# Twelve output pairs: issued in front of the second step, or left further behind

## The chip, the cores and the metric

The kernel runs on 1 core of one Trainium2 chip. The metric is device time in microseconds (us), the median of the fast runs where nothing else is said; the profile covers one execution and its span is some 2 us shorter than that execution's time. Executions are compared within the fast state only: two fell into a slow state (one of 1206.62 us, one profile at a granted clock of 0.754) and are left out. In the runs used the granted TensorE clock was 0.999 to 1.0.

## The reference, cut to what matters

```python
# attention part: per head a causal 7-tap convolution over the sequence, with softmaxed taps
out = np.einsum('hk,bskhg->bshg', softmax(weight), windows_of(x))     # 32768 tokens x 192
# second part
h = out @ w_in                      # 192 -> 2048
g = h / (1 + np.exp(-beta * h))     # Swish with one beta for each of the 2048 features
return g @ w_out                    # 2048 -> 192
```

## The kernel before

Work goes in 32 **steps** of 1024 tokens (two halves of 512), each of 16 **units** of 128 features. A unit u of step s does, on TensorE (PE), the *hidden* matmuls (6 of them, into the tile `ph`, of which there are two, in PSUM, the memory in which matmuls accumulate here), then a number of *output pairs*; ScalarE (ACT) turns `ph` into `g`; VectorE (DVE) convolves for a later step and evicts finished output accumulators (it adds up their two halves into the tile `osb`).

An output **job** is 256 tokens of a step's output: 32 pairs of matmuls (16 feature blocks x 2 blocks of 128 tokens) accumulate in one PSUM accumulator, `pa` or `pb`. There is exactly one of each. `ph` twice, `pa` and `pb`, of two 2 KiB banks each, are eight banks: all that the Trainium skill (PSUM — Partial Sum Buffer, Specifications (TRN2)) gives for PSUM, so a third accumulator of this size has no room; that the limit is eight was not tried here.

```python
class Job:
    def ready(self, s, u):
        fcs = NF if self.s < s else max(0, u - LAG + 1)   # LAG = 2: two units behind ScalarE
        return self.done < fcs * self.nb
    ...
    def leave(self):                                      # the eviction
        osb = osb_pool.tile([128, 2, D], FP32, name="osb")
        ...
        nc.vector.tensor_reduce(dst, self.po[:, :, 0 : nb * D].rearrange("p r n -> p n r"),
                                axis=mybir.AxisListType.X, op=ALU.add)
        ...  # then the store to HBM

def output(s, u, pairs, free):
    for _ in range(pairs):
        for name in free:                                 # a freed slot takes the next job
            if slots[name] is None and waiting:
                slots[name] = waiting.popleft()
        live = [(j.s, j.h, j.q, n) for n, j in slots.items() if j is not None]
        for *_, name in sorted(live):                     # the oldest job that is ready goes on
            job = slots[name]
            if job.ready(s, u):
                break
        else:
            return                                        # none ready: this unit gets fewer pairs
        if job.po is None:
            job.po = place[name]()                        # must wait until the last job there is evicted
        if job.pair():                                    # two matmuls; True: it was the last
            job.leave()
            slots[name] = None

for s in range(N_ST):
    jobs_of(s)                                            # 4 jobs, 128 pairs
    for u in range(NF):
        if s == 1 and u == 0:
            output(s, u, 12, "ab")                        # the early run that the change removes
        if s > 0 or u > 1:
            hidden(s, u)
        ...
        if s > 0:
            output(s, u, 8 if s < N_ST - 1 else 7, "ab")
        elif u > 8:
            output(s, u, 5, "ab")
        elif u > 2 and u not in CONV1:
            output(s, u, 4, "a")
        ...                                               # convolution taps, loads, casts
while waiting or any(slots.values()):                     # the tail
    output(N_ST, 0, 1, "ab")
```

A step creates 128 pairs and its 16 units issue 8 each, so the **backlog** (pairs created and not yet issued when a step ends) stays what it is, unless `ready` refuses.

Of the kernel before, what the change touches and what calls it, by code (L numbers as in the profile page):

```python
# [17 lines left out]
def kernel(  # L18
# [72 lines left out]
    def load(ch):  # L91
        p, c = divmod(ch, CHUNKS)
        xf = xf_pool.tile([128, 2, NB, D], FP32, name="xf")
        for h in range(2):
            nc.sync.dma_start(
                out=xf[:, h],
                in_=x_v[p, c * TOK : (c + 1) * TOK, h, :].rearrange(
                    "(b q) d -> q b d", q=BLK
                ),
            )  # L100
        xfs[ch] = xf

    def cast(ch, h):
        if h == 0:
            xbs[ch] = xb_pool.tile([128, NB, NG, 2, DG], BF16, name="xb")
        nc.vector.tensor_copy(  # L106
            xbs[ch][:, :, :, h, :],
            xfs[ch][:, h].rearrange("q b (p c) -> q b c p", c=NG),
        )
# [13 lines left out]
    def xpose(ch):  # L123
        xt = new_xt(ch)
        halo(ch, xts[ch - 1])
        for b in range(NB):
            nc.sync.dma_start_transpose(
                xt[:, :, HALO + b * BLK : HALO + (b + 1) * BLK],
                xbs[ch][:, b].rearrange("q c h p -> q (c h p)"),
            )  # L130
# [242 lines left out]
    def conv_ops(s, c0):  # L373
        def tap(k):
            if k == 0 and c0 == 0:
                new_ct(s)
            o = HALO - PAD + k
            src = xts[s][:, c0:, o : o + TOK]
            dst = cts[s][:, c0:, :]
            scalar = cw[:, k : k + 1]  # L380
            if k == 0:
                nc.vector.tensor_scalar_mul(dst, src, scalar)  # L382
            else:
                nc.vector.scalar_tensor_tensor(  # L384
                    out=dst, in0=src, scalar=scalar, in1=dst, op0=ALU.mult, op1=ALU.add
                )

        return [lambda k=k: tap(k) for k in range(K)]
# [3 lines left out]
    def hidden(s, fc, js=range(NG), ph=None):  # L392
        if fc == 0 and s not in gs:
            gs[s] = g_pool.tile([128, NF, 2, TOK], BF16, name="g")
        if ph is None:
            ph = psum_h.tile([128, 2, TOK], FP32, name="ph")
        for j in js:
            for h in range(2):
                rows = slice(h * DG, (h + 1) * DG)
                nc.tensor.matmul(  # L400
                    ph[:, h, :],
                    w_in_s[rows, j, fc * 128 : (fc + 1) * 128],
                    cts[s][rows, j, :],
                    start=(j == 0),
                    stop=(j == NG - 1),
                )
            if j == NG - 1:
                nc.scalar.activation(  # L408
                    gs[s][:, fc], ph, AF.Silu, scale=beta[:, fc : fc + 1]
                )  # L410
        return ph
# [59 lines left out]
    def jobs_of(s):  # L471
        for h in range(2):
            for q in range(0, NB, 2):
                if s == N_ST - 1 and h == 1 and q == NB - 2:
                    waiting.extend([Job(s, h, q, 1), Job(s, h, q + 1, 1)])
                else:
                    waiting.append(Job(s, h, q, 2))

    def output(s, u, pairs, free):
        for _ in range(pairs):  # L480
            for name in free:
# [4 lines that stand above are left out]
            for *_, name in sorted(live):  # L486
# [4 lines that stand above are left out]
                return  # L491
            if job.po is None:
                job.po = place[name]()
            if job.pair():
                job.leave()
                slots[name] = None
# [10 lines left out]
    for s in range(N_ST):  # L507
        jobs_of(s)
        at = 9 if s == 0 else 0
        for u in range(NF):  # L510
            if s == 1 and u == 0:
                output(s, u, 12, "ab")
            if s > 0 or u > 1:
                hidden(s, u)
            elif u == 0:
                phs = [hidden(0, fc, range(NG - 1)) for fc in range(2)]
                for fc in range(2):
                    hidden(0, fc, range(NG - 1, NG), phs[fc])
            if s == 0 and 0 < u < 4:
                next(second_work)  # L520
            if s == 0 and u in CONV1:
                next(conv1_work)
# [6 lines that stand above are left out]
            if s == 0 and u in first_work:  # L529
                first_work[u]()  # L530

            if s == 0 and u == min(CONV1):
                queue.extend(conv_ops(1, 1))
            pops = u % 2 if s > 0 else u in (4, 6, 7, 9, 11, 12, 13)
            if pops and queue:
                queue.popleft()()

            if u == at and s + 3 < N_CH:
                load(s + 3)
            if u == at and s + 2 < N_CH:  # L540
                cast(s + 2, 0)
            if u == at + 1 and s + 2 < N_CH:
                cast(s + 2, 1)
                xpose(s + 2)
            if u == 12 and s + 2 < N_CH:
                queue.extend(conv_ops(s + 2, 0))
# [32 lines left out]
```

## Time and profile before

| before | |
|---|---|
| time | 702.66 us, the middle of three runs, of which one was slow; the fast runs are 701.54 and 702.66 |
| span of the profile | 699.5 us |
| one unit in full swing | 1.308 us |
| one step (28 steps' mean) | 21.167 us; 16 units would be 20.93 |
| ScalarE per unit | 1.11 us of work, 0.19 us of waiting |

From the page of the kernel before: busy time by engine, the chain of waits that ended last by engine, and four groups of instructions (busy us, mean ns | idle us before, and what ended most of it). PEld is the loading of weights for TensorE, POOL is GpSimd, "issue" is time in which an engine waited for nothing that the profile shows, and ACTq is ScalarE's sequencer.

```profile
PE 690.4 (99%) x11300; PEld 518.3 (74%) x11300; DVE 519.5 (74%) x467; ACT 575.9 (82%) x525; POOL 6.5 (1%) x17
...
PE 92%; DVE 4%; ACT 2%; issue 1%; ACTq 0%
...
L408 ACT ACTIVATE g<-ph,beta 128x1024 bf16<-128x1024 f32 x512 | 569.5, 1114 | 106.1 <-PE ph L400 100.6
L433 PEld LDWEIGHTS <-g 64*128 64x128 bf16 x8160 | 367.7, 94 | 114.3 <-issue 11.2
...
L433 PE MATMUL pa<-w_out_s,g 64*128 64x192 bf16 x4112 | 240.0, 243 | 3.3 <-ACT g L408 1.1
...
L451 DVE TENSOR_REDUCE osb<-pa 128x384 f32<-128x768 f32 x64 | 61.0, 953 | 154.5 <-PE pa L433 154.5
```

PE bounds the kernel, and only 3.3 us of waiting are shown in front of `pa`'s matmuls. The timeline of the kernel before around the start of one step (start us, length us, engine, line, operation, count, then idle time in front):

```profile
351.66 0.51 PE L433 MATMUL pa<-w_out_s,g 64*128 64x192 bf16 x8
...
351.99 0.51 PE L433 MATMUL pb<-w_out_s,g 64*128 64x192 bf16 x8
352.21 0.96 DVE L451 TENSOR_REDUCE osb<-pa 128x384 f32<-128x768 f32 x1 [4.67 <-PE pa L433]
...
352.32 0.83 PE L400 MATMUL ph<-ct,w_in_s 64*128 64x512 bf16 x6
...
353.22 0.84 PE L433 MATMUL pa<-w_out_s,g 64*128 64x192 bf16 x16
353.22 0.60 PEld L433 LDWEIGHTS <-g 64*128 64x128 bf16 x15 [0.37 <-issue]
...
353.87 0.83 PE L400 MATMUL ph<-ct,w_in_s 64*128 64x512 bf16 x6
```

Read the starts, not the lengths. Hidden matmuls are followed by pairs 0.65 us after they start in the units around it; here 352.32 is followed by 353.22, which is 0.25 us late. The lengths overlap (the profile models the end of a matmul), so no idle time is shown in front of the matmuls. What the late one waits for is DVE's eviction of `pa`, from 352.21 to 353.17. The chain of waits of the kernel before, in order of time, says so too:

```profile
351.84 0.34 PE pa L433 x8
...
352.21 0.97 DVE osb L451
...
353.22 0.84 PE pa L433 x16
```

The chain counts the whole eviction, 0.97 us, of which 0.25 are lost.

The start of step 1, in the timeline of the kernel before:

```profile
32.13 0.34 PE L433 MATMUL pa<-w_out_s,g 64*128 64x192 bf16 x4
...
33.10 0.34 PE L433 MATMUL pa<-w_out_s,g 64*128 64x192 bf16 x4 [0.63 <-ACT g L408]
33.28 0.82 PE L433 MATMUL pb<-w_out_s,g 64*128 64x192 bf16 x16
...
33.94 0.81 PE L400 MATMUL ph<-ct,w_in_s 64*128 64x512 bf16 x6
...
34.79 1.11 ACT L408 ACTIVATE g<-ph,beta 128x1024 bf16<-128x1024 f32 x1 [1.75 <-PE ph L400]
```

The early run's first job needs the newest `g`; PE waits for ACT, the hidden matmuls of step 1 stand behind it, and then ACT waits 1.75 us for them. The Trainium skill (PSUM — Partial Sum Buffer, Engine vs sequencer instructions) says that matmuls start in program order; this trace agrees: the ready ones start at 33.94, behind the one that waited to 33.10.

### The profile page before, as it was taken

How to read it: one execution, taken by the hardware profiler on the slowest of the kernel's cores; microseconds unless marked ns; L12 is line 12 of the kernel's file. 1: busy time of each engine (PE TensorE's matmuls, PEld its weight loads, DVE VectorE, ACT ScalarE, POOL GpSimd, SP SyncE). 2: the span in 40 equal slices, each digit the busy share in tenths (PEclk: the TensorE clock that was granted, in tenths of full speed). 3: DMA queues.
4: the chain of work that ended last, by engine and by line, in shares of the span. 5: the costliest groups of instructions: out<-in, count | busy, mean ns of one | idle time of the engine just before them, and what ended most of it. 6: DMA issues, size and time to landing. Idle time of an engine off the chain costs nothing.

```text
span 699.5 us, 24308 instructions
## 1 busy us (share of the span) xinstructions
PE 690.4 (99%) x11300; PEld 518.3 (74%) x11300; DVE 519.5 (74%) x467; ACT 575.9 (82%) x525; POOL 6.5 (1%) x17
## 2 busy tenths in 40 slices
PE   8999999999999999999999999999999999999998
PEld 4677777777777777777777777777777777777776
DVE  5898877797777897777887777987777977778712
ACT  5788888888888888888888888888888888888884
POOL 3000000000000000000000000000000000000000
PEclk9999999999999999999999999999999999999999
DMA  9654322443322443323444423443323443232111
GB/s 212 173 115 115 87 89 73 98 114 107 94 75 75 110 115 100 95 75 76 115 114 99 93 65 89 115 115 86 104 58 98 115 109 87 75 80 65 47 36 58
DMA packets 121445, 66.86 MB, mean 96 GB/s; under 512 B 53232, under 2 KB 121344, under 8 KB 121344
## 3 DMA queue, kind: packets, MB, share of 16 engines
q1 hardware_dynamic: 119632, 63.73, 35.2%
q0 software_dynamic: 1664, 1.57, 1.4%
q8 instruction: 88, 1.44, 0.9%
q14 instruction: 13, 0.11, 0.1%
q10 hardware_dynamic: 48, 0.01, 0.0%
HBM read 29.89 MB, written 25.17 MB: 79 GB/s over the span
## 4 chain that ended last, share of the span: by engine, by line
PE 92%; DVE 4%; ACT 2%; issue 1%; ACTq 0%
PE ph L400 44%; PE pa L433 25%; PE pb L433 22%; DVE osb L451 4%; ACT g L408 2%; PE ph L274 1%; PE pb L274 0%; ACT xt L285 0%; PE pa L274 0%; DVE xt L342 0%; DVE w_out_s L301 0%; PE ph L226 0%; PE pb L243 0%; ACTq L153 0%; ACT L177 0%
## 5 line engine op out<-in xcount | busy, mean ns | idle before, releaser
L408 ACT ACTIVATE g<-ph,beta 128x1024 bf16<-128x1024 f32 x512 | 569.5, 1114 | 106.1 <-PE ph L400 100.6
L433 PEld LDWEIGHTS <-g 64*128 64x128 bf16 x8160 | 367.7, 94 | 114.3 <-issue 11.2
L400 PE MATMUL ph<-ct,w_in_s 64*128 64x512 bf16 x3072 | 423.0, 376 | 0.6 <-ACT g L408 0.6
L384 DVE SCALAR_TENSOR_TENSOR ct<-xt,cw,ct 128x1536 bf16<-128x1536 bf16 (+1 forms) x186 | 333.7, 1794 | 2.3
L433 PE MATMUL pa<-w_out_s,g 64*128 64x192 bf16 x4112 | 240.0, 243 | 3.3 <-ACT g L408 1.1
L433 PE MATMUL pb<-w_out_s,g 64*128 64x192 bf16 (+1 forms) x4048 | 225.4, 243 | 0.0
L400 PEld LDWEIGHTS <-w_in_s 64*128 64x128 bf16 x3072 | 157.3, 94 | 55.1 <-issue 1.8
L451 DVE TENSOR_REDUCE osb<-pa 128x384 f32<-128x768 f32 x64 | 61.0, 953 | 154.5 <-PE pa L433 154.5
L451 DVE TENSOR_REDUCE osb<-pb 128x384 f32<-128x768 f32 x63 | 60.0, 953 | 9.4 <-PE pb L433 7.6
L106 DVE CAST xb<-xf 128x768 bf16<-128x768 f32 x60 | 40.5, 674 | 0.3 <-DMA xf<-in_x_dram 0.3
L382 DVE TENSOR_SCALAR ct<-xt,cw 128x1536 bf16<-128x1536 bf16 (+1 forms) x31 | 30.7, 990 | 0.0
L226 PE MATMUL ph<-zeros 128*128 128x512 bf16 (+3 forms) x12 | 4.5, 476 | 1.3 <-DVE warm L176 1.3
L449 ACT COPY osb<-pb 128x192 f32<-128x192 f32 x1 | 0.3, 319 | 6.1 <-PE pb L433 6.1
L317 ACT ACTIVATE ct<-pa,rn 128x512 bf16<-128x512 f32 x1 | 0.7, 687 | 5.6 <-PE pa L274 5.6
L206 POOL DMA_DIRECT2D w_in_s<-in_moe_w_in_dram x8 | 5.1, 648 | 0.0
L121 DVE COPY xt<-xt 128x18 bf16<-128x18 bf16 x27 | 4.4, 162 | 0.0
L274 PE MATMUL ph<-xt,diag 128*128 128x512 f32 x14 | 3.5, 401 | 0.4 <-ACT xt L285 0.4
L315 DVE TENSOR_SCALAR ct<-ph,rn 128x512 bf16<-128x512 f32 x2 | 1.5, 750 | 3.1 <-PE ph L274 3.1
L301 DVE TENSOR_TENSOR w_out_s<-w_out_raw,beta_r 128x768 bf16<-128x768 f32 x4 | 3.8, 946 | 0.0
L274 PEld LDWEIGHTS ph<-xt,diag 128*128 128x128 f32 x14 | 2.5, 188 | 1.2 <-ACT xt L285 0.6
L342 DVE COPY xt<-pb 128x768 bf16<-128x768 bf16 x2 | 1.9, 958 | 1.5 <-PE pb L243 1.5
L226 PEld LDWEIGHTS <-zeros 128*128 128x128 bf16 x12 | 1.3, 123 | 2.1 <-DVE warm L176 1.3
(53 smaller groups left out, 28.0 us busy)
## 6 DMA issues: line engine op xcount, KB each, us to landing
out_dram<-osb SPq DMA_DIRECT2D x127, 192.0 KB, 2.0
xf<-in_x_dram SPq DMA_DIRECT2D x60, 384.0 KB, 4.4
xt<-xb SPq DMA_TRANSPOSE x120, 3.2
x<-in_x_dram SPq DMA_DIRECT2D x4, 384.0 KB, 5.1
w_in_s<-in_moe_w_in_dram POOLq DMA_DIRECT2D x8, 192.0 KB, 11.7
w_out_raw<-in_moe_w_out_dram SPq DMA_DIRECT2D x4, 384.0 KB, 15.3
out_dram<-osb SPq DMA_DIRECT2D x2, 96.0 KB, 1.6
cw<-in_weight_dram ACTq DMA_DIRECT2D x1, 0.2 KB
```

Of the source, the lines that this page charges most:

```text
L106: nc.vector.tensor_copy(xbs[ch][:, :, :, h, :], xfs[ch][:, h].rearrange("q b (p c) -> q b c p", c=NG),)
L121: nc.vector.tensor_copy(dst, last[:, :, HALO + TOK - PAD :])
L206: nc.gpsimd.dma_start(out=w_in_s[r * DG : (r + 1) * DG, :, cols], in_=w_in_v[:, :, cols])
L226: nc.tensor.matmul(pf[:, 0, 0:cols], zeros[:, 0:128], zeros[:, 0:cols], start=True, stop=True)
L274: nc.tensor.matmul(pv, diag[:, k, :], xt[:, o : o + TOK], start=(k == 0), stop=(k == K - 1))
L301: nc.vector.tensor_tensor(w_out_s[:, fcs, :], w_out_raw[:, fcs, :], beta_r[:, fcs].unsqueeze(2).to_broadcast((128, NQ, D)), ALU.mult,)
L382: nc.vector.tensor_scalar_mul(dst, src, scalar)
L384: nc.vector.scalar_tensor_tensor(out=dst, in0=src, scalar=scalar, in1=dst, op0=ALU.mult, op1=ALU.add)
L400: nc.tensor.matmul(ph[:, h, :], w_in_s[rows, j, fc * 128 : (fc + 1) * 128], cts[s][rows, j, :], start=(j == 0), stop=(j == NG - 1),)
L408: nc.scalar.activation(gs[s][:, fc], ph, AF.Silu, scale=beta[:, fc : fc + 1])
L433: nc.tensor.matmul(self.po[:, r, b * D : (b + 1) * D], g[rows, fc, self.h, q * BLK : (q + 1) * BLK], w_out_s[rows, fc, :], start=(self.don ...
L451: nc.vector.tensor_reduce(dst, self.po[:, :, 0 : nb * D].rearrange("p r n -> p n r"), axis=mybir.AxisListType.X, op=ALU.add,)
```

## The change

The 12 pairs in front of step 1 are not issued early; every later pair is issued as many places further behind the hidden matmuls.

```diff
         for u in range(NF):
-            if s == 1 and u == 0:
-                output(s, u, 12, "ab")
             if s > 0 or u > 1:
                 hidden(s, u)
```

## The prediction

> **What bounds it.** TensorE. The page has PE 99% busy at clock 0.999; the chain of waits is 92% PE. In time order a full unit of work (6 matmuls L400, then 8 output pairs L433) starts every 1.308 us (six starts from 358.44 to 366.29); ScalarE needs 1.11 us per unit and waits 0.19 us for PE each time; VectorE has idle time left (154.5 us waiting for pa). One output pair costs about 0.083 us (40 matmuls in 1.65 us in the tail).
>
> **What is not seen in the busy share.** A step of 16 units takes 21.167 us ((649.55 - 78.05) / 27), not 16 x 1.308 = 20.93. The missing 0.235 us is at one place: at 351.66 pa gets its last 4 pairs and pb its last 4 in the same unit; both accumulators are finished, hidden matmuls follow (0.65 us), and the next pa pair waits for the eviction of pa (352.21 to 353.17) and starts at 353.22 instead of 352.97. The chain shows it once per step as "DVE osb 0.97". The idle column misses it, since modelled matmul ends cover it; the Trainium skill (Perfetto Trace Analysis, Identifying the Most-Contended Engine) calls matmul busy time a bad measure for this reason, and the trace agrees.
>
> **Why.** I counted the issue order. Before, the 12 early pairs leave the backlog so small that in step 1 the rule "two units behind" starves the last units (7 and 4 pairs instead of 8), and the backlog locks at 72 pairs per step end, where both first jobs of a step end together in unit 0 of the next. Without the 12, the backlog stays at 79: 8 pairs in every unit; pa ends in unit 0 and pb still has 4 + 7 pairs. So between pa's last pair and its reuse lie 0.33 + 0.65 + 0.58 = 1.56 us, where the eviction took 1.23 us from end to restart (351.99 to 353.22). No other accumulator change of the step is closer. The pair that reads the newest g (units 14, 15) stands where it stood.
>
> **Cost.** Matmuls, evictions, bytes: unchanged; only order. The tail gets 7 pairs longer (95 instead of 88, +0.58 us), which is work taken from before it, so not a loss. Gains, all on PE:
> - 28 stalls of 0.235 us at the starts of steps 2 to 30 and one of about 0.24 at 670.72: 6.8 us
> - end of step 1: waits 0.24 before 56.00 (ACT) and 0.23 before 56.88: 0.5 us
> - start of step 1: PE waits 0.8 us for ACT at 32.3 to 33.10, in front of the hidden matmuls, so ACT idles 1.75 us. After, hidden(1,0) goes first (its input is ready at 31.95), the wait shrinks to about 0.15: 0.65 us
> Sum 7.9 us, 1.1%.
>
> **Prediction.** 702.66 - 7.9 = 694.8 us; range 692.5 to 698.5. Faster by over 2%: 0.02; within 2%: 0.97; slower by over 2%: 0.01. In direction: almost surely faster.
>
> **Right if:** step period 20.93 us in time order; "DVE osb" gone from the chain but for start and end; pa wait after hidden matmuls near zero; backlog steady; span near 691.6; ACT idle near 33.04 gone; tail after the last activation about 0.6 us longer. PE, DVE and ACT busy sums equal within 1%.
>
> **Wrong if:** DVE evicts pa late (behind a conv tap, or the order of casts and evictions moved to unit 1 makes DVE late), so that the 0.33 us slack is eaten: then the stall returns at unit 1 of each step and the gain falls towards 1 us; or if changing between pa and pb costs something that the unit times of before don't show; or ct of step 1 is not ready at 32.1, so PE waits there.

## The result, and the profile after

694.43 us (693.34 to 694.69, four fast runs) against 701.54, the median of the three fast runs of the kernel before (701.29 to 702.66): ratio 0.9892, 95% interval 0.9872 to 0.9911. Executions over 1.5% slower than the fastest of the same kernel are left out of the means. Ratios here are the mean time of one kernel's fast runs over that of the other's of the same rounds, so they are not quite the ratio of the quoted medians. The span is 691.4 us. The predicted 694.8 us (691.6 us of span) was right; it is clearly faster.

The same lines of the page after, but for the eviction's:

```profile
PE 685.2 (99%) x11300; PEld 496.3 (72%) x11300; DVE 524.4 (76%) x467; ACT 576.1 (83%) x525; POOL 6.5 (1%) x17
...
PE 98%; ACT 1%; issue 0%; DVE 0%; ACTq 0%
...
L408 ACT ACTIVATE g<-ph,beta 128x1024 bf16<-128x1024 f32 x512 | 569.6, 1114 | 97.1 <-PE ph L400 91.5
L433 PEld LDWEIGHTS <-g 64*128 64x128 bf16 x8160 | 353.0, 94 | 120.7 <-ACT g L408 0.9
...
L433 PE MATMUL pa<-w_out_s,g 64*128 64x192 bf16 x4112 | 238.6, 243 | 0.5 <-ACT g L408 0.5
```

PE's busy share is 99% in both pages, although 8 us of waiting have gone. What tells are the chain (DVE 4% to 0%) and the idle time of the weight loads, where the 11.2 us of "issue" are no longer the largest item (0.9 us for ACT is). The start of the same kind of step after, PE's timeline:

```profile
346.25 0.81 PE L400 MATMUL ph<-ct,w_in_s 64*128 64x512 bf16 x6
346.89 0.49 PE L433 MATMUL pa<-w_out_s,g 64*128 64x192 bf16 x8
347.23 0.49 PE L433 MATMUL pb<-w_out_s,g 64*128 64x192 bf16 x8
347.56 0.81 PE L400 MATMUL ph<-ct,w_in_s 64*128 64x512 bf16 x6
348.20 0.74 PE L433 MATMUL pb<-w_out_s,g 64*128 64x192 bf16 x14
348.78 0.25 PE L433 MATMUL pa<-w_out_s,g 64*128 64x192 bf16 x2
348.86 0.81 PE L400 MATMUL ph<-ct,w_in_s 64*128 64x512 bf16 x6
```

`pa` ends in the first unit as before, but `pb` has 7 pairs (14 matmuls) left for the second. They fill the time of the eviction, and `pa` is taken up at 348.78 with no gap. From hidden to hidden: 347.56 - 346.25 = 1.31 and 348.86 - 347.56 = 1.30, all units alike.

The start of step 1 after:

```profile
32.27 0.83 PE L400 MATMUL ph<-ct,w_in_s 64*128 64x512 bf16 x6
...
32.92 0.67 PE L433 MATMUL pa<-w_out_s,g 64*128 64x192 bf16 x8
...
33.42 0.49 PE L433 MATMUL pb<-w_out_s,g 64*128 64x192 bf16 x8
...
34.61 1.11 ACT L408 ACTIVATE g<-ph,beta 128x1024 bf16<-128x1024 f32 x1 [0.35 <-PE ph L400]
```

The hidden matmuls go first and ACT's wait before the second activation of the step is 0.35 us.

**A measure without the start-up.** The first 23 us hold the loads and the first convolution, and vary from run to run. So the table below also gives the *stretch*, from the ACT start after its wait of about 0.5 us in step 0 (23.55 us before, 23.69 after; from 23.43 to 25.09 in all the profiles) to the start of ACT's last copy (696.58 and 688.43). It repeats to 0.01 us: 664.74 for the changed kernel in two profiles on two occasions.

The stretch fell by 673.03 - 664.74 = 8.29 us.

### The profile page after: what moved, and what is told of

The parts are those of the page before. It is cut to its first block, busy times and chain, and to the rows that moved or that the text cites. A ratio compares the mean times of both kernels' runs of the same rounds, so it can differ in the third digit from the quotient of the medians.

```text
span 691.4 us, 24308 instructions
## 1 busy us (share of the span) xinstructions
PE 685.2 (99%) x11300; PEld 496.3 (72%) x11300; DVE 524.4 (76%) x467; ACT 576.1 (83%) x525; POOL 6.5 (1%) x17
## 4 chain that ended last, share of the span: by engine, by line
PE 98%; ACT 1%; issue 0%; DVE 0%; ACTq 0%
PE ph L400 48%; PE pa L433 25%; PE pb L433 24%; PE ph L274 1%; ACT g L408 0%; PE pb L274 0%; PE pa L274 0%; PE pb L243 0%; PE ph L226 0%; ACT xt L285 0%; DVE xt L342 0%; DVE w_out_s L301 0%; ACTq L153 0%; ACT L177 0%; PE pb L231 0%
## 5 line engine op out<-in xcount | busy, mean ns | idle before, releaser
L433 PEld LDWEIGHTS <-g 64*128 64x128 bf16 x8160 | 353.0, 94 | 120.7 <-ACT g L408 0.9
L400 PE MATMUL ph<-ct,w_in_s 64*128 64x512 bf16 x3072 | 415.3, 376 | 0.6 <-ACT g L408 0.6
L400 PEld LDWEIGHTS <-w_in_s 64*128 64x128 bf16 x3072 | 142.0, 94 | 62.8 <-issue 1.8
```

Of the source, the lines that this page charges most:

```text
L400: nc.tensor.matmul(ph[:, h, :], w_in_s[rows, j, fc * 128 : (fc + 1) * 128], cts[s][rows, j, :], start=(j == 0), stop=(j == NG - 1),)
L433: nc.tensor.matmul(self.po[:, r, b * D : (b + 1) * D], g[rows, fc, self.h, q * BLK : (q + 1) * BLK], w_out_s[rows, fc, :], start=(self.don ...
```

## The experiments

All were correct. "Backlog" is counted from the issue order; "pairs of pb" are those left to `pb` after `pa` ends, in the same unit and the next; a step is the mean over 28 steps, from one eviction of `pa` to the same one later.

| kernel | backlog | pairs of pb | step, us | stretch, us | span, us | ratio to before, 95% |
|---|---|---|---|---|---|---|
| before | 72 | 4 + 0 | 21.167 | 673.03 | 699.5 | 1 |
| after | 79 | 4 + 7 | 20.92 | 664.74 | 691.4 | 0.9892 (0.9872 to 0.9911) |
| mid4 (profile of mid4look) | 75 | 4 + 3 | 20.92 | 664.77 | 691.7 | 0.9885 (0.9869 to 0.9902) |
| mid6 | 73 | 4 + 1 | 21.08 | 669.65 | 696.1 | 0.9954 (0.9939 to 0.9969) |
| mid12 | 72 | 4 + 0 | 21.17 | 672.39 | 699.1 | 0.9995 (0.9978 to 1.0011) |
| start12back | 79 | 4 + 7 | 20.92 | 665.39 | 691.8 | 0.9892 (0.9877 to 0.9907) |
| behind4 | 83 | 4 + 8 + 3 | 20.92 | 664.74 | 691.4 | 0.9884 (0.9869 to 0.9898) |
| twice | 79 | 4 + 7 | 21.59 | 684.78 | 711.1 | 1.0170 (1.0154 to 1.0185) |
| ends | 79 | 4 + 7 | 20.92 | 664.43 | 690.9 | 0.9873 (0.9856 to 0.9889) |
| ends2 | 79 | 4 + 7 | 20.92 | 663.94 | 691.9 | 0.9877 (0.9862 to 0.9891) |
| after_again | 79 | 4 + 7 | 20.92 | 664.74 | 691.4 | 0.9877 (0.9860 to 0.9893) |

The step of twice is taken from one step, 56.96 - 35.37 us. Three theories are told apart. **Accumulator**: the second accumulator must have pairs enough left to cover the eviction of the first. **Backlog**: each pair further behind the hidden matmuls brings its share. **Start of step 1**: all was gained where the early run stood.

### mid4: four pairs back, after the start of step 1

```diff
-                output(s, u, 8 if s < N_ST - 1 else 7, "ab")
+                output(s, u, (8 if s < N_ST - 1 else 7) + (1 if s == 1 and 2 <= u < 6 else 0), "ab")
```

> Changed kernel plus 4 extra output pairs in the middle of step 1 (units 2 to 5 get 9), so the backlog at every later step end is 75 instead of 79, and pb has 4 + 3 pairs left when pa ends. Theory accumulator (the second accumulator must have enough pairs left to cover the eviction of the first): between pa's end and its reuse lie 0.33 + 0.65 + 0.25 = 1.23 us, just what the eviction takes, so no stall or one of a few hundredths per step: span 691.4 to 692.2, ratio about 0.989. Rival backlog (each pair further behind brings its share, 7 pairs 8 us): 4 of 7 pairs taken back give back 4.5 us, span about 696. Rival start of step 1 (all gained where the early run stood): 691.4.

The time was 693.15 us (three fast runs), ratio 0.9885: nothing was given back.

> The same kernel as mid4, whose profile fell in the slow state: one more profile. Accumulator: step period 20.93 to 20.95, pa restarts with no wait in unit 1 or one of a few hundredths, span 691.4 to 692.2.

This is a single execution (693.72 us, clock 1.0), among the fast runs of mid4 (693.13 to 694.40). PE's timeline at the start of a step:

```profile
348.21 0.83 PE L400 MATMUL ph<-ct,w_in_s 64*128 64x512 bf16 x6
348.86 0.43 PE L433 MATMUL pb<-w_out_s,g 64*128 64x192 bf16 x6
349.11 0.59 PE L433 MATMUL pa<-w_out_s,g 64*128 64x192 bf16 x10
349.52 0.83 PE L400 MATMUL ph<-ct,w_in_s 64*128 64x512 bf16 x6
```

Three pairs of `pb` (0.25 us) from 348.86 end at 349.11, and there `pa` starts. The stretch is 664.77 us, 0.03 more than the changed kernel's. Four of the seven pairs can go for nothing, which the backlog theory does not allow.

### mid6: six pairs back

The edit is that of mid4 with `2 <= u < 8`.

> The same with 6 extra pairs: backlog 73, pb has 4 + 1 left. Accumulator: 1.06 us lie between, the eviction takes 1.23, a stall of 0.17 us in each of 29 steps: step period 21.09 us, span about 696.3. Backlog: 6 of 7 given back, about 698.2. Start of step 1: 691.4.

The step took 21.08 us and the span 696.1. PE's timeline:

```profile
349.81 0.51 PE L433 MATMUL pb<-w_out_s,g 64*128 64x192 bf16 x8
350.14 0.83 PE L400 MATMUL ph<-ct,w_in_s 64*128 64x512 bf16 x6
350.79 0.26 PE L433 MATMUL pb<-w_out_s,g 64*128 64x192 bf16 x2
351.04 0.75 PE L433 MATMUL pa<-w_out_s,g 64*128 64x192 bf16 x14
351.61 0.83 PE L400 MATMUL ph<-ct,w_in_s 64*128 64x512 bf16 x6
```

One pair of `pb` (0.083 us) starts at 350.79, so `pa` could start at 350.87; it starts at 351.04, when its eviction is done. The unit takes 351.61 - 350.14 = 1.47 us instead of 1.31: 0.16 us lost in each step. Neither the idle column of the matmuls nor the chain (98% PE, DVE 0%) shows it. The starts do, and the weight loads, in the page of mid6 and in its timeline:

```profile
L433 PEld LDWEIGHTS <-g 64*128 64x128 bf16 x8160 | 368.4, 94 | 110.2 <-issue 4.7
...
351.04 0.52 PEld L433 LDWEIGHTS <-g 64*128 64x128 bf16 x13 [0.15 <-issue]
```

The 4.7 us are near the 669.65 - 664.74 = 4.91 us that the stretch lost.

### mid12: all twelve back, but not at the start

The edit is that of mid4 with `2 <= u < 14`.

> The changed kernel's start of step 1, but the 12 pairs are caught up in units 2 to 13 of step 1: the backlog locks at 72 as in the kernel before, both accumulators end in unit 0 of every step. Accumulator: the stall of 0.235 us is back in each step, period 21.17, and the starved units at the end of step 1 too: span about 698.8. Backlog: 698 to 699 as well. Start of step 1: nothing comes back, 691.4.

The step is 21.17 us and the time 701.09: nearly all the gain is lost again, although the start of step 1 is that of the changed kernel. The stretch is 673.03 - 672.39 = 0.64 us shorter than before: that is what the start of step 1 is worth.

### start12back: the early run kept, but paid back within step 1

```diff
 # kernel before, with its early run of 12
-                output(s, u, 8 if s < N_ST - 1 else 7, "ab")
+                output(s, u, (8 if s < N_ST - 1 else 7) - (1 if s == 1 and 2 <= u < 14 else 0), "ab")
```

> The kernel before with its early run of 12 pairs, paid back at once: units 2 to 13 of step 1 get 7 pairs instead of 8, so from step 2 on the order is that of the changed kernel (backlog 79). Accumulator: step period 20.93, only the loss at the start of step 1 (0.65 us) stays: span about 692.0. Backlog: the same. Start of step 1: everything stays lost, 699.5.

The step is 20.92 us and the time 693.94. The early run itself costs the stretch 665.39 - 664.74 = 0.65 us, the same number from the other side. These two crossed runs split the gain: 0.65 us at the start of step 1, the rest in what the backlog does to all later steps.

### behind4: four pairs further behind still

The edit is that of start12back in the changed kernel, with `2 <= u < 6`.

> Changed kernel with 4 pairs fewer in step 1 (units 2 to 5 get 7): backlog 83, so pb has 4 + 8 + 3 pairs left when pa ends. Accumulator: the eviction was covered already, nothing more to gain: step period 20.93, span 691.2 to 691.8 (before, in runs so far, 699.5). Rival backlog (each further pair brings its share, 1.1 us): 687.

The stretch is 664.74 us, the same to the hundredth. Further behind is no gain once the eviction is covered. The backlog theory falls.

### twice: the suspected cost doubled

```diff
-                nc.vector.tensor_reduce(dst, ...)
+                for _ in range(2 if self.h == 0 and self.q == 0 else 1):
+                    nc.vector.tensor_reduce(dst, ...)
```

> Changed kernel, but the eviction of the first job of each step (the one in pa that ends in unit 0) is done twice, the same result written again: VectorE gets 0.87 us more per step, which it has to spare (it waited 150 us for PE). Accumulator: eviction to restart grows from 1.23 to 2.10 us, 1.56 are covered, so PE waits 0.54 us at the end of unit 1 of each step: step period 21.47, span about 707.5, ratio 1.011. Backlog, or VectorE load off the critical path: 691.4 to 692.

The stall appeared where it was expected, and larger: span 711.1 instead of 707.5. Its timeline:

```profile
357.18 1.95 DVE L452 TENSOR_REDUCE osb<-pa 128x384 f32<-128x768 f32 x2 [3.44 <-PE pa L433]
...
357.95 0.74 PE L433 MATMUL pb<-w_out_s,g 64*128 64x192 bf16 x14
...
359.18 0.26 PE L433 MATMUL pa<-w_out_s,g 64*128 64x192 bf16 x2 [0.49 <-DVE osb L452]
```

I had added 0.87 us, the distance between the starts of two evictions of different accumulators (352.21 and 353.08 before). Two evictions of the same accumulator to the same place took 1.95 us together, 0.99 more than the 0.96 of one. `pa` could have started at 357.95 + 0.58 = 358.53 and started at 359.18: 0.65 us for each step, and 30 x 0.65 = 19.5 us, near the 684.78 - 664.74 = 20.04 measured. DVE was at 77% and had time to spare; what counts is when it ends this one instruction.

### ends and ends2: can the two waits that are left be taken away?

In the changed kernel PE still waits for ACT's newest `g` in two places: 0.2 us at the start of step 1, 0.47 in the tail. (0.47 is from the idle column; by the starts it is more: two pairs from 679.65 end at 679.82, and the next start at 680.44, 0.62 later.) In each, `pb` has pairs whose `g` is long ready.

```diff
+                if s == 1 and u == 0:
+                    output(0, NF, 4, "ab")          # two of pa, two of pb, then the rest
-                output(s, u, 8 if s < N_ST - 1 else 7, "ab")
+                output(s, u, 4 if s == 1 and u == 0 else 8 if s < N_ST - 1 else 7, "ab")
...
+    output(N_ST - 1, NF, 20, "ab")                  # ends: two of pa, 18 of pb; ends2: 12, so 10 of pb
     while waiting or any(slots.values()):
```

> Changed kernel with two orders mended: in unit 0 of step 1 and in the tail, pb's pairs whose g is long ready go in front of pa's last two pairs, which wait for ScalarE's newest g. In the changed kernel PE waits 0.47 us there in the tail and about 0.2 at step 1. Expected: span 690.7 to 690.9 instead of 691.4, ratio to before 0.9875 to 0.9885; no change in the steps between. If PE's wait there is not on the critical path: 691.4.

The stretch shrank by 664.74 - 664.43 = 0.31 us, less than the 0.5 to 0.7 expected. The tail in the timeline of ends shows why:

```profile
679.48 1.66 PE L433 MATMUL pb<-w_out_s,g 64*128 64x192 bf16 x36
680.97 0.34 PE L433 MATMUL pa<-w_out_s,g 64*128 64x192 bf16 x4
681.13 0.92 PE L433 MATMUL pb<-w_out_s,g 64*128 64x192 bf16 x18
...
682.36 2.82 PE L433 MATMUL pa<-w_out_s,g 64*128 64x192 bf16 x64 [0.31 <-DVE osb L451]
```

The wait for ACT is gone, but with 18 of `pb`'s pairs moved in front only 9 (18 matmuls, 0.74 us) are left behind `pa`'s end. They could be done at 681.13 + 0.74 = 681.87; the next `pa` starts at 682.36. I had rebuilt the very stall of the kernel before. So ends2 moves 10 only:

> The kernel 'ends' took 20 pairs in front in the tail, 18 of pb. That left 9 pairs of pb (0.74 us) between pa's end and its reuse, and the trace showed PE waiting 0.48 us there for the eviction: the wait on ScalarE was only changed into a wait on VectorE. Here 12 are taken in front, 10 of pb (0.83 us), which still covers ScalarE's last g; 17 of pb (1.40 us) stay behind pa's end and cover the eviction's 1.23 us. Accumulator: both waits gone, 0.48 us less than 'ends': span 690.4. If the order in the tail doesn't matter: 690.9.

> The changed kernel unaltered, beside ends2 on one chip: span 691.4 to 692.7 as in its earlier runs; ends2 should be 0.9 to 1.1 us shorter.

```profile
681.87 0.34 PE L433 MATMUL pa<-w_out_s,g 64*128 64x192 bf16 x4
682.04 1.57 PE L433 MATMUL pb<-w_out_s,g 64*128 64x192 bf16 x34
...
683.44 2.81 PE L433 MATMUL pa<-w_out_s,g 64*128 64x192 bf16 x64
```

This timeline of ends2 has no gap: 682.04 + 17 pairs x 0.083 = 683.45. The stretch is 663.94 us, 0.49 shorter than that of ends and 0.80 shorter than the changed kernel's, which fits 0.62 in the tail and 0.2 at step 1. But the span is 691.9 against 691.4 for after_again, and the ratios are equal (0.9877): in this profile the stretch began 1.35 us later (25.09 against 23.74), before anything that was edited, and that swallowed the 0.8 us. What was expected of the span failed; what was expected of the tail held. As a faster kernel ends2 is not shown: its total cannot be told from the changed kernel's with these runs.

## Why the prediction was right

- **Total.** 7.9 us were predicted to go; the means of the fast runs (701.83 and 694.23) differ by 7.6 us, the stretch by 8.29. The 702.66 us that the prediction started from was the slowest of the fast runs; 7.9 us off their mean would have been 693.9, at least as near to what was measured.
- **The stall at each step's start** was the main term, 6.8 us by 0.235 us a step. The step went from 21.167 to 20.92, so 0.25 a step; over 28 steps 6.9 us. It was the eviction of `pa` with too little PE work to cover it: mid4, mid6 and mid12 put 3, 1 and 0 pairs of `pb` into the second unit and lost 0.00, 0.16 and 0.25 us a step, and twice brought a stall back by a longer eviction alone.
- **Its cause, counted from the issue order** (the early run drives the backlog to the lowest value that "two units behind" allows, 72: two waiting jobs of 32 pairs and the last 4 pairs of the two in the accumulators, so that both accumulators end in one unit) is borne out by start12back and mid12, which have the early run without the locked backlog and the reverse.
- **The start of step 1**: 0.65 us predicted, 0.65 and 0.64 measured by the two crossed runs. PE's wait shrank as said; ACT's idle time did not vanish but fell from 1.75 to 0.35 us.
- **The end of step 1** (0.5 us predicted) was not isolated by a run. The trace of the kernel before gives it by the starts: the hidden matmuls of unit 2 start at 36.55 in step 1 and at 57.54 in step 2, 20.99 us apart, where 16 groups of hidden matmuls and the 123 pairs issued between them would take about 20.5 at the pace of full swing (1.308 us for a unit, 0.083 for a pair). So about 0.5 us were lost. At 670.72, 0.26 were lost (one pair of `pb` from 670.38 ends at 670.46). The terms add up: 0.65 + 6.9 + 0.5 + 0.26 = 8.3, against 8.29.
- **The tail** should get 0.6 us longer: from the last wait for ACT to the last copy it is 696.58 - 689.17 = 7.41 us before and 688.43 - 680.44 = 7.99 after.
- **Busy sums** within 1%: PE 690.4 to 685.2, DVE 519.5 to 524.4, ACT 575.9 to 576.1. PE's weight loads were not named, and changed by 4% (518.3 to 496.3).
- None of the three risks came true: DVE evicted in time, a change between `pa` and `pb` cost nothing that shows, and the input of step 1 was ready.

## What to carry to other kernels

With two accumulators and one eviction engine, look at when the two end relative to each other: the one that ends first is free again only after its eviction, and the other must still have that much matmul work (here 1.23 us from last pair to restart). A small burst early in a steady loop can set that phase for the whole run, so count the issue order of a whole run before moving work, and compare the period of the loop with the sum of its parts rather than trust a 99% busy share. An order that fills one wait must be checked against the wait it uncovers next.

## What the Trainium skill lacked or had wrong

- Perfetto Trace Analysis, Identifying the Most-Contended Engine, says that matmul busy time is not a good measure of how close a kernel is to roofline, and the runs agree: 99% both before and after 8 us of waiting went. It offers MFU (the matmul work over the time) and the busy share of LDWEIGHTS instead; the second does not follow the time here. It was 74% before (699.5 us of span), 72% after (691.4) and 75% in mid4look (691.7), and the sums differ by 4% (496.3 and 516.1 us) between two kernels of equal speed.
- The same page does not say that a short wait of PE can be missing from the idle time in front of matmuls and from the chain of waits alike, nor that the idle time of the weight loads can show it: in mid6 0.16 us a step, 4.9 us of the stretch, showed in neither of the first two, but in the starts of the matmuls and as 4.7 us in front of the weight loads.
- No page read has the time from an accumulator's last matmul to its reuse: 1.23 us here (351.99 to 353.22), for an eviction of 128x768 fp32 to 128x384 that took 0.96 us by itself; nor that two such evictions start 0.87 us apart when they have different accumulators, and take 1.95 us together when the second reads and writes the same tiles again.
